# Attention backward core on one core: head-0 scores issued one unit ahead into the spare PSUM bank, and the transposes and projections moved from even to odd units

## Chip, cores, metric

The kernel runs on one core of a Trainium2 chip. The metric is the device time of one execution in microseconds (us), as the median of several executions. Engines are named as in the profile: PE is TensorE, ACT is ScalarE, DVE is VectorE, POOL is GpSimd, and SP issues DMAs. A ratio between two kernels is the mean time of one kernel's fast runs over that of the other's fast runs of the same rounds, so it isn't quite the ratio of the medians quoted beside it.

## Reference

Two attention blocks share one call; the reference returns the output and all gradients. Only the second block (B) matters here: multi-query attention with 16 query heads, one key/value head, and head width 28 (padded to 32 in the kernel).

```python
def _B_ref(x, wq, wk, wv, wo):               # B, S, D = 1, 2048, 448; H = 16; Dh = 28
    q = (x @ wq).reshape(B, S, H, Dh).transpose(0, 2, 1, 3)
    k = x @ wk                                # one head, shared
    v = x @ wv
    scores = jnp.einsum("bhqd,bkd->bhqk", q, k) * (Dh ** -0.5)
    p = softmax(scores)
    o = jnp.einsum("bhqk,bkd->bhqd", p, v)
    return o.transpose(0, 2, 1, 3).reshape(B, S, H * Dh) @ wo
# ... block A (linear attention) ...
_out, _vjp = jax.vjp(_f, ...)                 # output and eight gradients, bfloat16
```

## The kernel before

Block B's core is a loop over 512 units and 28 more to drain it. Eight units make a *group*: 256 query rows times two heads, against all 2048 keys; a unit takes 256 keys. In unit `u` the forward part works on unit `u` (scores, exp) and the backward part on unit `w = u - 16` (dP, dS). Scores have three PSUM banks (`SB`; a bank is a 128x512 piece of the memory that PE writes its results to), used in rotation: two for the two heads of a unit, and one spare. dP has two (`DB`). In the profile they are called `sps` and `dps`. Names with d are gradients: dq, dk, dv and do those of q, k, v and the head output o, dP and dS those of the probabilities and the scores.

```python
def rows_SD(u, sp, dp):                       # scores (k=0) and dP (k=1), two heads, two halves each
    # ...
    todo = [(0, 0), (0, 1), (1, 0), (1, 1)] * 2
    if sp is not None and dp is not None and u % 2 == 0:
        todo = [(0, 0), (0, 1), (1, 0)] * 2 + [(1, 1)] * 2
    # ... each one is a matmul of 32 rows x 128 columns, on row group r

def out_part(u):
    n, q_ = (u % 64 - 24) // 8, u // 64 - 1   # a quarter of an output projection in some units 0 mod 8
    # ...

for u in range(NU + 28):                      # program order is issue order on each engine
    sp = [SB[(2 * u + h) % 3] for h in range(2)] if hasS else None
    dp = DB if hasD else None
    spare = SB[(2 * u + 2) % 3] if hasS else SB[2]
    rows_SD(u, sp, dp)
    if (b := due(u, 10)) is not None:         # units 2 mod 8
        onat_T(b, spare)                      # transposes of o into the spare bank
    if (b := due(u, 14)) is not None:         # units 6 mod 8
        don_T(b, spare)                       # transposes of do
    if op := out_part(u):
        out_proj(*op, spare)                  # projection
    # ... do projections in some units, also into the spare bank
    ACT:  exp head 0 -> eT
    DVE:  dsT head 0 = dP head 0 * eT;  ACT: cp = copy(dP head 1);  POOL: dsT head 1 = cp * eT
    # ... DVE and POOL read the transposes out: o_norm, row_D, don_copy, out_store
    ACT:  exp head 1 -> eT;  every second unit: SP: DMA transpose eN <- eT
    if u % 2:
        dk_m(...)                             # 16 matmuls, odd units
    else:
        o_dq(...)                             # o and dq, even units
        for n in {4: (0,), 6: (1, 2), 0: (3,)}.get(u % 8, ()):
            dv_mm(...)                        # dv, reads eN
    DVE:  dsx <- transpose(dsT)
```

The three names ACT, DVE and POOL in front of a line are shorthand of this text for the engine call that stands there. "Extra" below means any of the things that use the spare bank: transposes of o, transposes of do, a projection.

## Time and profile before

| | before |
|---|---|
| time, median of 4 runs | 1110.22 us (1110.05 to 1111.34) |
| first exp of unit 0, of unit 64, of unit 511 | 227.3, 332.7, 1027.9 us |
| units 64 to 511 | 695.1 us |
| one group (8 units) late in the core, with / without a projection | 12.56 / 12.19 us |

The unit times are worked out from the starts of the exp of head 0 in the timeline (ACT instruction of line 861). The averages of the last row are over units 192 to 503.

The page's head and part 1 give the span and each engine's busy time, share and instruction count:

```profile
span 1106.9 us, 39147 instructions
...
PE 1044.4 (94%) x15645; PEld 484.3 (44%) x15645; DVE 897.9 (81%) x1772; ACT 881.4 (80%) x1744; POOL 757.3 (68%) x986
```

The timeline of ACT, one group, only the exp of head 0 of units 304 to 312 (columns: start in us, duration in us, engine, line, instruction, and in brackets the idle time before it and what ended it). Between two shown lines stand the copy and the exp of head 1.

```profile
707.70 0.62 ACT L861 ACTIVATE eT<-sps 128x512 bf16<-128x512 f32 x1
...
709.55 0.60 ACT L861 ACTIVATE eT<-sps 128x512 bf16<-128x512 f32 x1 [0.25 <-PE dps L625]
...
711.00 0.62 ACT L861 ACTIVATE eT<-sps 128x512 bf16<-128x512 f32 x1
...
712.68 0.60 ACT L861 ACTIVATE eT<-sps 128x512 bf16<-128x512 f32 x1
...
714.12 0.62 ACT L861 ACTIVATE eT<-sps 128x512 bf16<-128x512 f32 x1
...
715.72 0.60 ACT L861 ACTIVATE eT<-sps 128x512 bf16<-128x512 f32 x1
...
717.17 0.62 ACT L861 ACTIVATE eT<-sps 128x512 bf16<-128x512 f32 x1
...
718.86 0.60 ACT L861 ACTIVATE eT<-sps 128x512 bf16<-128x512 f32 x1
...
720.30 0.62 ACT L861 ACTIVATE eT<-sps 128x512 bf16<-128x512 f32 x1
```

Read the differences. From an odd to an even unit it is 1.45 us each time: ACT starts its three instructions 0.48 us apart and waits for nothing. From an even to an odd unit it is 1.85 us after a projection (707.70 to 709.55), 1.68 after the transposes of o, 1.60 with no extra, 1.69 after the transposes of do. The bracket names a dP matmul: the profile puts the wait down to the last matmul of the set, and the score matmuls stand just before it in the same set.

Why even to odd is longer can be seen in the timeline of PE, in unit 306, with its transposes of o (line 744; `oq` is the bank of o and dq):

```profile
710.43 0.28 PE L625 MATMUL sps<-R,R 32*128 32x256 bf16 x2
...
710.55 0.50 PE L625 MATMUL dps<-doT,R 32*128 32x256 bf16 x3
711.18 0.33 PE L744 MATMUL sps<-identF,oTs 64*128 64x64 f32 x2
711.44 0.29 PE L625 MATMUL oq<-eT,R 128*32 128x256 bf16 x2
...
712.26 0.28 PE L625 MATMUL sps<-R,R 32*128 32x256 bf16 x2 [0.21 <-DVE oTs L754]
```

The transposes start at 711.18 although the rows of the unit were issued by 710.8: they wait for the spare bank, which the exp of head 1 of the unit before still reads until 711.12. Then come the transposes (0.26 us to the next start), o and dq, and a wait of 0.21 us until DVE has read the transposes out. Only then can the next unit's scores (712.26) use that bank, and ACT gets them 0.42 us later. An extra in an even unit is thus a chain: release of the bank, extra, o and dq, next scores. Which end of it binds differs: after the transposes of o, it is DVE's read-out (it ends at 1.22 us from the unit's exp, the scores start at 1.27; medians of units 192 to 503); after the other two extras DVE is done 0.2 us before the scores start, so PE's own work (o, dq and dv) is taken to bind.

The waits from 250 to 1030 us (who waited for whom, total us, times, longest):

```profile
PEld sps L744 <- ACT eT L899: 24.7, 62, 0.4
ACT eT L861 <- PE dps L625: 18.9, 45, 6.9
PE sps L625 <- DVE oTs L754: 13.2, 61, 0.5
...
PE dv_acc L625 <- DMA eN<-eT: 6.5, 1, 6.5
```

The last line is a single stall of 6.5 us: the first dv matmuls wait for a DMA transpose. The busy times by stretch show it and what follows (columns: stretch, its length, busy us and count of each engine, granted PE clock, DMA share, GB/s):

```profile
257.00:260.00 3.00, 0.26 (x7) 0.00 (x0) 1.05 (x3) 1.03 (x3) 2.22 (x3) 1.00 1.69 113
260.50:267.50 7.00, 3.73 (x45) 1.64 (x48) 2.28 (x5) 2.57 (x6) 1.15 (x1) 0.51 1.04 185
```

PE is idle, and from 260.5 us, still inside the stall, it gets half its clock for 7 us. The Trainium skill, "TensorE: Matmul & The Clock Gate" (Part 1: The HAM clock gate), says that the clock is halved after an idle window of about 3.4 us and returns after about as long a busy one; here the stall is longer than such a window and the clock reads 0.51.

### The profile page before, as it was taken

The numbers are of one execution on the slowest core, as the hardware profiler recorded it, in microseconds if no ns is written. First come the engines' busy times: TensorE is split into PE (matmuls) and PEld (weight loads), VectorE is DVE, ScalarE is ACT, GpSimd is POOL, SyncE is SP. The second block draws the span as 40 slices with busy tenths as digits, with TensorE's granted clock in tenths as the row PEclk, the third lists the DMA queues.
The fourth block names the chain that finished last, engine by engine and source line by source line (L and its number), as shares of the span: only waits on it lengthen the run. The fifth ranks groups of instructions, "written<-read, shape, count | busy, mean of one in ns | idle before, by whom it ended". The sixth has DMA issues, their size and how long they took to land.

```text
span 1106.9 us, 39147 instructions
## 1 busy us (share of the span) xinstructions
PE 1044.4 (94%) x15645; PEld 484.3 (44%) x15645; DVE 897.9 (81%) x1772; ACT 881.4 (80%) x1744; POOL 757.3 (68%) x986
## 2 busy tenths in 40 slices
PE   9999999997999999999999999999999999999998
PEld 5545555443444444444444444444444444444344
DVE  7886400436999999999999999999999999999942
ACT  6454122567999999999999999999999999999621
POOL 6001252325888888888888888888888888888840
PEclk9999999988999999999999999999999999999999
DMA  9869899199999999999999999999999999999962
GB/s 267 143 131 185 176 181 216 39 200 168 192 192 191 187 188 199 187 187 189 180 192 191 185 184 187 192 191 190 187 204 186 178 185 192 194 171 178 206 138 63
DMA packets 672535, 199.01 MB, mean 180 GB/s; under 512 B 649585, under 2 KB 668321, under 8 KB 672353
## 3 DMA queue, kind: packets, MB, share of 16 engines
q1 hardware_dynamic: 660512, 175.19, 98.2%
q0 software_dynamic: 6880, 17.37, 6.5%
q10 hardware_dynamic: 4960, 3.96, 1.2%
q8 instruction: 122, 2.00, 0.7%
q14 instruction: 61, 0.49, 0.1%
HBM read 21.00 MB, written 12.94 MB: 31 GB/s over the span
## 4 chain that ended last, share of the span: by engine, by line
PE 53%; DVE 29%; ACT 7%; issue 6%; DMA 4%; POOL 0%; SPq 0%; DVEq 0%; ACTq 0%; POOLq 0%
PE agen L80 13%; PE dk_acc L625 11%; DVE dsx L931 11%; DVE dsT L866 9%; PE sps L80 6%; ACT eT L899 5%; PE oq L625 5%; PE sps L625 4%; PE aacc L80 4%; PE dps L625 3%; PE dv_acc L625 3%; DVE R L884 2%; DVE oTs L881 2%; DMA eN<-eT 2%; DVE oTs L754 2%
## 5 line engine op out<-in xcount | busy, mean ns | idle before, releaser
L869 POOL TENSOR_TENSOR dsT<-cp,eT 128x512 bf16<-128x512 bf16 x512 | 588.1, 1155 | 122.1 <-ACT cp L868 114.6
L866 DVE TENSOR_TENSOR dsT<-dps,eT 128x512 bf16<-128x512 f32 x512 | 343.4, 671 | 27.8 <-PE dps L625 22.7
L931 DVE STREAM_TRANSPOSE dsx<-dsT 128x512 f32<-128x512 f32 x512 | 357.7, 699 | 2.1
L861 ACT ACTIVATE eT<-sps 128x512 bf16<-128x512 f32 x512 | 311.8, 609 | 37.4 <-PE dps L625 18.9
L625 PEld LDWEIGHTS <-R 32*128 32x128 bf16 (+1 forms) x8192 | 197.9, 94 | 304.5 <-issue 272.5
L868 ACT ACTIVATE cp<-dps 128x512 bf16<-128x512 f32 x512 | 312.8, 611 | 11.5 <-PE dps L625 10.4
L899 ACT ACTIVATE eT<-sps 128x512 bf16<-128x512 f32 x512 | 319.0, 623 | 0.0
L625 PE MATMUL dk_acc<-dsx,qX 32*32 32x512 bf16 x4096 | 267.6, 375 | 0.0
L625 PE MATMUL dps<-doT,R 32*128 32x256 bf16 x2048 | 252.7, 270 | 13.0 <-DVE dsT L866 7.7
L625 PE MATMUL sps<-R,R 32*128 32x256 bf16 x2048 | 217.5, 274 | 14.9 <-DVE oTs L754 13.2
L625 PE MATMUL oq<-eT,R 128*32 128x256 bf16 x2048 | 158.3, 276 | 0.0
L625 PE MATMUL oq<-dsT,R 128*32 128x256 bf16 x2048 | 157.5, 275 | 0.1
L625 PEld LDWEIGHTS <-qX 32*32 32x32 bf16 x4096 | 79.7, 89 | 114.8 <-issue 54.2
L625 PE MATMUL dv_acc<-eN,don 128*32 128x512 bf16 x1024 | 96.9, 379 | 6.5 <-DMA eN<-eT 6.5
L80 PEld LDWEIGHTS <-R 128*128 128x128 bf16 (+1 forms) x553 | 45.8, 99 | 46.1 <-issue 18.7
L396 POOL MEMSET ga<- 64x448 bf16 x2 | 0.9, 470 | 93.4 <-DVE pr L347 80.0
L546 DVE TENSOR_TENSOR osb<-R 32x512 bf16<-32x512 bf16 x4 | 1.6, 412 | 62.1 <-ACT R L543 62.1
L625 PEld LDWEIGHTS <-don 128*32 128x32 bf16 x1024 | 33.8, 97 | 0.3
L80 PE MATMUL agen<-R,R 128*128 128x448 bf16 x128 | 28.6, 352 | 0.7 <-ACT R L219 0.5
L874 POOL DMA_DIRECT2D qX<-qn_d x32 | 18.1, 569 | 16.4 <-PE dps L80 16.4
L884 DVE TENSOR_SCALAR R<-oq 64x256 bf16<-64x256 f32 x64 | 27.3, 427 | 2.0
L499 ACT ACTIVATE wdq<-agen 128x448 bf16<-128x448 f32 x16 | 8.7, 543 | 24.9 <-PE agen L80 24.9
(220 smaller groups left out, 1023.5 us busy)
## 6 DMA issues: line engine op xcount, KB each, us to landing
qX<-qn_d POOLq DMA_DIRECT2D x32, 256.0 KB, 6.2
eN<-eT SPq DMA_TRANSPOSE x256
out_dram<-osb ACTq DMA_DIRECT2D x22, 112.0 KB
qn_d<-gaT SPq DMA_DIRECT2D x2, 1024.0 KB
xa<-in_A_x_dram SPq DMA_DIRECT2D x8, 224.0 KB
ga<-in_grad_out_dram SPq DMA_DIRECT2D x4, 448.0 KB
xa<-in_grad_out_dram POOLq DMA_DIRECT2D x4, 448.0 KB, 6.9
out_dram<-wdq POOLq DMA_DIRECT2D x8, 224.0 KB, 3.6
```

The lines of the kernel that those rows point to most:

```text
L80: nc.tensor.matmul(out_ap, lhsT=lhsT, rhs=rhs, start=start, stop=stop, tile_position=(0, 0))
L625: nc.tensor.matmul(out, lhsT=lhsT, rhs=rhs, start=start, stop=stop, tile_position=pos, skip_group_check=True)
L754: nc.vector.tensor_tensor(out=os_, in0=onp[:, :, :, :], in1=r_[:].to_broadcast([P, 2, 2, 32]), op=ALU.mult)
L861: nc.scalar.activation(out=et[:, u % 2, 0, :], in_=sp[0][:, :], func=ACT.Exp, scale=scale)
L866: nc.vector.tensor_tensor(out=dst[:, 0, :], in0=dp[0][:, :], in1=ew[:, w % 2, 0, :], op=ALU.mult)
L868: nc.scalar.activation(out=cp[:, :], in_=dp[1][:, :], func=ACT.Copy)
L869: nc.gpsimd.tensor_tensor(out=dst[:, 1, :], in0=cp[:, :], in1=ew[:, w % 2, 1, :], op=ALU.mult)
L874: nc.gpsimd.dma_start(qX[qc][32 * a:32 * a + 32, :, :, :].rearrange("j b s c -> j b (s c)"), qn_d[qc * 256:(qc + 1) * 256, :].rearrange("( ...
L881: nc.vector.tensor_copy(out=oTs[0:64, :], in_=oq[0:64, 0:256])
L884: nc.vector.tensor_scalar(out=qT_B[g][64 * hp:64 * hp + 64, qc * 256:(qc + 1) * 256], in0=oq[64:128, 0:256], scalar1=scale, scalar2=None, ...
L899: nc.scalar.activation(out=et[:, u % 2, 1, :], in_=sp[1][:, :], func=ACT.Exp, scale=scale)
L931: nc.vector.transpose(out=dsx[b][:, tp, :, :, :].rearrange("p h t c -> p (h t c)").bitcast(F32), in_=dsT[y][:, :, :].rearrange("p h c -> p ...
```

## The change

Intent: while an even unit runs, the head-0 scores of the next, odd unit are put into the spare bank, so ACT always has an exp to do when PE is late. The spare bank must then be free in even units, so everything else that uses it moves to odd units. The early loads of qX and wo and the do projections are re-timed as well.

```diff
-        def rows_SD(u, sp, dp):
+        def rows_SD(u, sp, dp, early, ahead):
+            todo = []
+            if sp is not None:
+                todo += [(0, u, 1)] if early else [(0, u, 0), (0, u, 1)]
+            if dp is not None:
+                todo += [(1, w, 0), (1, w, 1)]
+            todo *= 2
+            if dp is not None and sp is not None and u % 2 == 0:
+                todo = [d for d in todo if d != (1, w, 1)] + [(1, w, 1)] * 2
+            if ahead is not None:
+                todo += [(0, u + 1, 0)] * 2
... (out_part: units 1 mod 8 instead of 0 mod 8)
-        free = [*range(1, 16), *range(17, 27, 2), *range(32, 64, 8), ...]
+        free = [*range(1, 16), *range(17, 27, 2), *range(29, 65, 4), 65, 69, 73]
...
-                rows_SD(u, sp, dp)
-                if (b := due(u, 10)) is not None:
+                op = out_part(u)
+                dpj = do_slots.pop(u, None)
+                taken = op or due(u, 11) is not None or due(u, 15) is not None or dpj is not None and u >= 27
+                ahead = spare if u + 1 < NU and not taken else None
+                rows_SD(u, sp, dp, early, ahead)
+                early = ahead is not None
+                if (b := due(u, 11)) is not None:
                     onat_T(b, spare)
-                if (b := due(u, 14)) is not None:
+                if (b := due(u, 15)) is not None:
                     don_T(b, spare)
...
-                for a in {2: (0, 2), 8: (1, 3)}.get(u, ()) ...      # first qX loads
+                for a in {10: (0, 2), 18: (1, 3)}.get(u, ()) ...
-                if u == 12:
+                if u == 44:
                     nc.gpsimd.dma_start(wo, ...)
... (row_D 12 -> 13, o_norm 10 -> 11, don_copy 14 -> 15; the qT copy after o_norm)
```

Units 3 (o) and 7 (do) mod 8 are always taken, and unit 1 mod 8 where a projection falls in. In those units no early score is issued.

## The prediction

> **What bounds it now.** The attention core (512 units, first exp of unit 0 at 227 us, of unit 511 at 1028 us) is 800 of 1110 us. In the timeline a unit is three ScalarE instructions (exp head 0, copy, exp head 1), started 0.48 us apart: 1.45 us per unit, 11.6 us per eight units. Measured: 12.5-12.66 us per eight with an output projection, 12.13-12.24 without. TensorE sets the difference. The unit-to-unit intervals show it: odd to even is always 1.45 us (ScalarE-bound), even to odd is 1.68 (after the transposes of o), 1.70 (of do), 1.88 (projections): the extra work in an even unit delays the next unit's first scores. Besides, the waits list one stall of 6.5 us near 257 us: the first dv matmuls wait for transposing DMAs, while four qX loads and the wo load share the DMA engines.
>
> **What the change does, costed.**
> (a) Even units are always "ahead", so even to odd falls to about 1.45-1.55 us. Gain in eight units: about 0.6 us, 1.0 with a projection.
> (b) Extras now stand in odd units, before the dk matmuls, and take the spare bank, so there is no early score for the next unit. That bank is released by exp head 1 of the unit before, 0.19 us after the unit's own first exp starts. Then run: extra (0.26 o; about 0.35 do with one more mode switch; 0.47 projection), dk 0.975, scores to exp 0.43. Odd to even becomes about 1.85, 2.0-2.1 and 2.06 us instead of 1.45. Loss: 1.0 us in eight units, 1.6 with a projection. In even units only o/dq followed (0.45-0.55), not dk.
> (c) The early scores wait, in TensorE's order, for exp head 1 of the unit before. TensorE now leads ScalarE by 0.4-0.7 us; in odd "ahead" units it will stand still about 0.4-0.5 us and start the next extra later. Two serial matmuls on one row group also add 0.1 us per ahead unit.
> (d) Half of the first qX loads and wo are issued later: most of the 6.5 us stall goes.
>
> The Trainium skill, "TensorE: Matmul & The Clock Gate" (The mechanism), says that matmuls keep strict order: this is why (c) blocks. "TensorEngine Tiling" (Key Properties) says that changing tiling mode drains the engine: the trace agrees, with about 0.2 us between rows, transposes and dk.
>
> Following these waits by hand through eight units reproduces before (12.08 against 12.13-12.24) and gives after about 12.8 us without and 13.3 with a projection (estimates from the durations above). Over 62 such groups that is +36 to +41 us, less 5-6 us for (d).
>
> **Predicted: 1142 us, range 1114 to 1162; faster by over 2%: 0.14, within 2%: 0.22, slower by over 2%: 0.64.**
>
> **What would show each step.** (a) Even-to-odd intervals near 1.45-1.55. (b) Odd-to-even intervals of 1.85-2.1 at the extras, with ScalarE's first exp waiting for scores there; 1.45 elsewhere. (c) In the waits, TensorE's score matmuls waiting for the head-1 exp, tens of us in total; the projections and transposes of o waiting for it too. (d) No 6.5 us dv wait near 257 us.
>
> **What would make it wrong.** If TensorE falls behind ScalarE for good, the early scores never block and the gain (a) dominates: at TensorE's own sum of about 11.8-12.3 us per eight, the time is near 1085. If the do transposes need no extra switch, the loss shrinks. If the eT-to-eN transposing DMAs, which are up to 18 us late early on, bind, less changes. VectorE (about 11.3 us of 12.5 occupied) could also hide part.

## The result

| | before | after |
|---|---|---|
| time, median of 4 runs | 1110.22 us | 1143.12 us (1141.21 to 1144.3) |
| ratio of fast runs, 95% interval | | 1.0292 [1.0275, 1.031] |
| first exp of unit 0 | 227.3 | 229.5 |
| units 0 to 64 | 105.4 | 106.5 |
| units 64 to 511 | 695.1 | 726.6 |
| rest to the end | 79.0 | 79.9 |
| one group, with / without a projection | 12.56 / 12.19 | 13.29 / 12.67 |

Nearly all of the loss, 31.5 us of 35.7 us between the two profiled runs, lies in units 64 to 511: 0.72 us in each group with a projection and 0.48 without (averages over units 192 to 503).

Units 0 to 64 took 1.1 us longer, but that is a sum of larger parts. The third group, which had a DMA stall before, gained 7.0 us; the five groups after it lost 5.9; and the first group lost 2.3 (14.19 us against 11.88). In that first group PE got half its clock for 13.6 us, against 6.9 before. This length varies from trace to trace (3.4 us in four of the twelve, 6.8 in six, 10.3 and 13.6 in one each), and the first group takes 10.7, 11.9 to 12.1, 13.0 and 14.2 us with it. So the 2.3 us can't be put down to the change.

The page's head and part 1 of the kernel after:

```profile
span 1142.6 us, 38986 instructions
...
PE 1099.7 (96%) x15645; PEld 510.1 (45%) x15645; DVE 913.5 (80%) x1772; ACT 879.6 (77%) x1744; POOL 760.6 (67%) x986
```

PE, the engine with the higher share, became busier by 55 us with the same number of matmuls. That isn't 55 us of new work: durations are modelled and overlapping ones are merged here. Matmuls that used to run side by side (dP and both scores) now stand partly one behind the other, but that can't be all of it: the run without early scores further below, where no scores are put ahead, is still at 1070.3 us, 26 more than before. The busy time of PE therefore doesn't tell what the change costs; the unit times do.

The timeline of ACT, the same units 304 to 312, exp of head 0 (now line 870):

```profile
727.03 0.60 ACT L870 ACTIVATE eT<-sps 128x512 bf16<-128x512 f32 x1 [0.38 <-PE dps L625]
...
728.48 0.62 ACT L870 ACTIVATE eT<-sps 128x512 bf16<-128x512 f32 x1
...
730.58 0.60 ACT L870 ACTIVATE eT<-sps 128x512 bf16<-128x512 f32 x1 [0.50 <-PE dps L625]
...
732.03 0.62 ACT L870 ACTIVATE eT<-sps 128x512 bf16<-128x512 f32 x1
...
733.93 0.60 ACT L870 ACTIVATE eT<-sps 128x512 bf16<-128x512 f32 x1 [0.30 <-PE dps L625]
...
735.38 0.62 ACT L870 ACTIVATE eT<-sps 128x512 bf16<-128x512 f32 x1
...
738.34 0.60 ACT L870 ACTIVATE eT<-sps 128x512 bf16<-128x512 f32 x1
...
740.31 0.60 ACT L870 ACTIVATE eT<-sps 128x512 bf16<-128x512 f32 x1 [0.38 <-PE dps L625]
```

Now even to odd is 1.45 us, as intended. (The first experiment shows that moving the extras out of the even units is enough for that; the early scores aren't needed.) (Unit 310, at 736.81, is left out by the cut, so 735.38 to 738.34 are two units.) But odd to even after an extra is 2.10 (projection), 1.90 (o), 1.97 (do). Averages over units 192 to 503, in us, groups with a projection:

| from unit to unit, mod 8 | 0-1 | 1-2 | 2-3 | 3-4 | 4-5 | 5-6 | 6-7 | 7-0 | sum |
|---|---|---|---|---|---|---|---|---|---|
| before | 1.84 | 1.45 | 1.69 | 1.45 | 1.53 | 1.45 | 1.70 | 1.45 | 12.56 |
| after | 1.45 | 2.10 | 1.45 | 1.91 | 1.45 | 1.43 | 1.53 | 1.97 | 13.29 |

The timeline of PE in unit 307, which has the transposes of o (now line 749), answers to the one of unit 306 before; the last three lines are unit 309, which has early scores and is read further below:

```profile
731.73 0.36 PE L625 MATMUL dps<-doT,R 32*128 32x256 bf16 x2
732.21 0.34 PE L749 MATMUL sps<-identF,oTs 64*128 64x64 f32 x2
732.48 1.04 PE L625 MATMUL dk_acc<-dsx,qX 32*32 32x512 bf16 x16
733.45 0.28 PE L625 MATMUL sps<-R,R 32*128 32x256 bf16 x2
...
735.24 0.28 PE L625 MATMUL dps<-doT,R 32*128 32x256 bf16 x2
735.55 0.37 PE L625 MATMUL sps<-R,R 32*128 32x256 bf16 x2
735.86 0.61 PE L625 MATMUL dk_acc<-dsx,qX 32*32 32x512 bf16 x8
```

Behind the transposes stands dk with 0.97 us instead of o and dq with about 0.5 us and a wait of 0.2. From the start of the transposes to the next scores it was 1.08 us; it is 1.24 us. ACT gets the scores at 733.93, 0.48 us after their start.

The waits from 250 to 1062 us:

```profile
ACT eT L870 <- PE dps L625: 54.3, 148, 0.5
...
PEld sps L749 <- ACT eT L908: 23.9, 62, 0.4
...
PE dps L625 <- DVE dsT L875: 3.2, 15, 0.2
```

ACT's wait for PE grew from 18.9 us in 45 waits (of which 6.9 were the DMA stall) to 54.3 in 148. The wait of dv for the DMA is gone, and so is the half clock in that stretch:

```profile
257.00:260.00 3.00, 2.76 (x30) 1.40 (x30) 2.71 (x7) 3.00 (x8) 2.37 (x3) 1.00 1.27 169
260.50:267.50 7.00, 6.45 (x106) 3.13 (x109) 6.69 (x14) 6.70 (x14) 6.92 (x11) 1.00 1.11 189
```

The third group (units 16 to 24) takes 12.36 us instead of 19.40.

### The profile page after: what moved, and what is told of

It reads as the page before. It is cut to its first block, busy times and chain, and to the rows that moved or that the text cites. A ratio compares the mean times of both kernels' runs of the same rounds, so it can differ in the third digit from the quotient of the medians.

```text
span 1142.6 us, 38986 instructions
## 1 busy us (share of the span) xinstructions
PE 1099.7 (96%) x15645; PEld 510.1 (45%) x15645; DVE 913.5 (80%) x1772; ACT 879.6 (77%) x1744; POOL 760.6 (67%) x986
## 4 chain that ended last, share of the span: by engine, by line
PE 62%; ACT 15%; DVE 13%; issue 8%; DMA 1%; DVEq 0%; ACTq 0%
PE dk_acc L625 17%; PE agen L80 12%; PE sps L625 10%; ACT cp L877 6%; ACT eT L908 6%; PE sps L80 5%; DVE dsx L940 5%; PE aacc L80 4%; DVE dsT L875 4%; PE oq L625 3%; PE dps L625 3%; PE dv_acc L625 2%; DVE R L899 2%; PE dps L80 2%; ACT eT L870 1%
## 5 line engine op out<-in xcount | busy, mean ns | idle before, releaser
L875 DVE TENSOR_TENSOR dsT<-dps,eT 128x512 bf16<-128x512 f32 x512 | 350.1, 684 | 54.2 <-PE dps L625 45.8
L625 PEld LDWEIGHTS <-R 32*128 32x128 bf16 (+1 forms) x8192 | 222.0, 94 | 334.7 <-issue 318.0
L870 ACT ACTIVATE eT<-sps 128x512 bf16<-128x512 f32 x512 | 314.4, 614 | 64.5 <-PE dps L625 54.3
L877 ACT ACTIVATE cp<-dps 128x512 bf16<-128x512 f32 x512 | 310.8, 607 | 12.5 <-PE dps L625 12.3
L625 PE MATMUL sps<-R,R 32*128 32x256 bf16 x2048 | 311.0, 273 | 8.1 <-DVE R L586 0.8
L625 PE MATMUL dps<-doT,R 32*128 32x256 bf16 x2048 | 225.2, 271 | 12.8 <-DVE dsT L875 4.5
L625 PE MATMUL dv_acc<-eN,don 128*32 128x512 bf16 x1024 | 90.9, 379 | 0.0
L80 PEld LDWEIGHTS <-R 128*128 128x128 bf16 (+1 forms) x553 | 46.1, 100 | 46.5 <-issue 18.9
L763 POOL TENSOR_TENSOR prod<-R,oTs 128x128 f32<-128x128 bf16 x64 | 27.7, 433 | 2.0 <-DVE oTs L759 2.0
L625 PEld LDWEIGHTS <-don 128*32 128x32 bf16 x1024 | 28.1, 97 | 0.6
```

The costliest lines, as they stand in the source:

```text
L80: nc.tensor.matmul(out_ap, lhsT=lhsT, rhs=rhs, start=start, stop=stop, tile_position=(0, 0))
L625: nc.tensor.matmul(out, lhsT=lhsT, rhs=rhs, start=start, stop=stop, tile_position=pos, skip_group_check=True)
L763: nc.gpsimd.tensor_tensor(out=prod[b][:], in0=dnv, in1=os_, op=ALU.mult)
L870: nc.scalar.activation(out=et[:, u % 2, 0, :], in_=sp[0][:, :], func=ACT.Exp, scale=scale)
L875: nc.vector.tensor_tensor(out=dst[:, 0, :], in0=dp[0][:, :], in1=ew[:, w % 2, 0, :], op=ALU.mult)
L877: nc.scalar.activation(out=cp[:, :], in_=dp[1][:, :], func=ACT.Copy)
```

## The experiments

The theory: the loss is made by the place of the extras (dk now stands behind them), with a smaller part by the early scores, which wait in PE's order. Rival A: the early scores make it all. Rival B: the early scores help, and the place loses more than the whole. The runs below were made on two chips, each with the kernel before beside it. In them, the kernel before itself scatters (1103.7 to 1118.3 us in seven fast runs of the first call, the longest with the lowest mean granted clock, 0.987), so time ratios under about 1% don't say much. The unit intervals inside a trace do: where a kernel's instructions were the same, their averages agreed with those of the first pair within 0.03 us, mostly within 0.01. The table of unit times at the end of this section uses them.

### The change without its early scores

```diff
-                ahead = spare if u + 1 < NU and not taken else None
+                ahead = None
```

> The change without its early scores: transposes and projections stay in odd units. My theory (loss shared by position of the extras and early scores): following the waits gives 12.9 us in eight units with a projection and 12.3 without, about 0.3 less than the change, so 1122 to 1128 us; odd-to-even intervals at the extras still 1.8 to 2.1 us. Rival A (the early scores make the whole loss): 1102 to 1108 us. Rival B (the position makes the loss, and the early scores win some of it back): slower than the change, 1150 us or more.

Measured: 1135.2 us against 1107.34 of before, ratio 1.0233 [1.0182, 1.0284]; correct. The intervals at the extras are 2.10 (projection), 1.90 (o) and 1.84 (do), nearly those of the change; a group takes 13.19 and 12.57 us. The time missed the expected 1122 to 1128 us. The timeline of ACT, the exp of head 0 of units 305 to 308 (between them stand the copy and the exp of head 1):

```profile
722.74 0.61 ACT L870 ACTIVATE eT<-sps 128x512 bf16<-128x512 f32 x1
...
724.83 0.60 ACT L870 ACTIVATE eT<-sps 128x512 bf16<-128x512 f32 x1 [0.50 <-PE dps L625]
...
726.29 0.61 ACT L870 ACTIVATE eT<-sps 128x512 bf16<-128x512 f32 x1
...
728.17 0.60 ACT L870 ACTIVATE eT<-sps 128x512 bf16<-128x512 f32 x1 [0.29 <-PE dps L625]
```

Even to odd (724.83 to 726.29) is short here too: 1.46, 1.46, 1.51 and 1.48 us on average.

So the place of the extras alone costs 0.63 and 0.38 us per group, and the early scores 0.10 on top (13.29 less 13.19, 12.67 less 12.57). Rival A falls. Rival B falls too, since taking the early scores out made it no slower: units 64 to 511 take 721.3 us against 726.6. (The two time ratios to before, 1.0233 and 1.0292, are too close for their intervals to settle this.) The theory's split was wrong in size: about 0.3 was expected for the early scores, and 0.3 less for the place of the extras.

### Before, with the early scores only

```diff
+                taken = op or due(u, 10) is not None or due(u, 14) is not None or dpj is not None and u >= 27
+                ahead = spare if u + 1 < NU and not taken else None
+                rows_SD(u, sp, dp, early, ahead)          # rows_SD of the change; extras stay in even units
```

> Before, with early scores wherever the spare bank is free; extras stay in even units. My theory: the early scores alone lose, by standing in TensorE's order until the head-1 exp has read the bank and by two serial matmuls: 12.8 us in eight units with a projection, 12.65 without, so 1128 to 1136 us. Rival A (early scores make the whole loss): 1140 us or more. Rival B (early scores help): 1110 us or less.

Measured: 1120.58 us, ratio 1.0103 [1.0048, 1.0157]; correct. A group takes 12.69 us with and 12.63 without a projection, against 12.56 and 12.19. Early scores lose by themselves, by 0.13 and 0.44 us per group, less in time than expected. Part of the difference may be that the profiled run had no long stall near 257 us (0.7 us, against 6.5 in before's trace), although its loads were the old ones.

Here the early scores stand in odd units and make the *next*, even unit with its extra start later: the interval 6 to 7 is 1.93 us instead of 1.70 and, in groups without a projection, 2 to 3 is 2.07 instead of 1.66.

### Half of dk left out, in both kernels (result wrong)

```diff
-                        for m in range(2 * i, 2 * i + 4):
+                        for m in (2 * i, 2 * i + 3):
                             dk_m(b, m)
```

In the change:

> The change with every second dk matmul group left out (the dk result is wrong on purpose); dk takes 0.43 us less in each odd unit. If the dk stretch stands between an extra and the next scores (my theory), the odd-to-even intervals at the extras shrink by that: projection 2.10 to about 1.67, o transposes 1.91 to 1.48, do transposes 1.97 to 1.54, all others stay near 1.45; about 12.0 us in eight units with a projection and 11.8 without, near 1076 us. Rival (the stall is the wait for the bank and its eviction, or ScalarE itself): these intervals stay within 0.1 us.

In the kernel before:

> Before with the same half of dk left out (dk wrong on purpose). My theory: before, dk ends ahead of the even unit and is hidden behind ScalarE, and the extra then waits for the bank (head-1 exp), so the even-to-odd intervals at the extras stay within 0.1 us of 1.84 (projection), 1.69 (o), 1.70 (do): 12.3 to 12.6 and 11.9 to 12.2 us in eight units, at most 12 us faster than before. Rival (TensorE's total work binds both kernels): about 1.7 us less in eight units, 100 us faster.

Measured: the change with half of dk 1110.08 us against 1111.18 of before, ratio 1.000 [0.9948, 1.0053]; the kernel before with half of dk 1104.57 us, 0.9951 [0.9898, 1.0003]. Only one output was wrong in both, the gradient of wk, which is made from dk. The change with half of dk missed its expectation (near 1076 us).

| | units 64 to 511, us | 1-2 (projection) | 3-4 (o) | 7-0 (do) |
|---|---|---|---|---|
| after | 726.6 | 2.10 | 1.91 | 1.97 |
| after, half of dk | 699.9 | 1.85 | 1.66 | 1.99 |
| | | 0-1 (projection) | 2-3 (o) | 6-7 (do) |
| before | 695.1 | 1.84 | 1.69 | 1.70 |
| before, half of dk | 695.2 | 1.85 | 1.70 | 1.70 |

This is the sharpest of the runs. The same 0.43 us less of dk per odd unit is worth 26.7 us in the change and nothing before. Before, dk stood where PE had time to spare; the change put it between an extra and the scores that ACT waits for.

But the theory's sizes were wrong: in groups with a projection, the projection and o intervals fell by 0.25, not 0.43 (o in the other groups by 0.16), and do didn't fall. In the half-dk run the waits from 300 to 1030 us have a line that the change doesn't have:

```profile
PE sps L625 <- DVE doT L787: 14.8, 53, 0.4
```

With dk shorter, the next scores wait until DVE has copied the transposed do out of the bank. In the change, dk hid that. The same bound stands behind the other two extras, though the waits don't list it: in the half-dk run the next scores start 0.05 us after DVE's read-out has ended (projection: 1.38 and 1.33 us from the unit's exp; o: 1.19 and 1.13; medians of units 192 to 503), in the change 0.3 us after it.

### Half of dk, with the copy of do ahead of the multiply on DVE

```diff
                 if (b := due(u, 15)) is not None:
                     don_T(b, spare)
+                    don_copy(b)              # taken from its place after the dsT multiply
```

> The change with half of dk (wrong on purpose), and VectorE copies the transposed do out before the unit's dsT multiply instead of after it. In the half-dk run the interval 7 to 0 stayed at 1.94 to 1.99 us while the other two fell by 0.25. If that is because the eviction of do by VectorE, which stands behind the multiply, holds the bank (so dk hid it in the change), the interval falls to 1.5 to 1.65 us. Rival: something else holds unit 0's scores (dO multiply, don on GpSimd), it stays at 1.9 or more.

Measured: 1118.74 us, ratio 1.0083 [1.0035, 1.0131]. The expectation was missed: interval 7 to 0 rose to 2.15 us. The timeline of units 311 and 312, all engines, shows why:

```profile
725.89 0.28 DVE L787 COPY doT<-sps 64x256 bf16<-64x256 bf16 x1 [0.51 <-PE sps L780]
...
726.10 0.67 DVE L876 TENSOR_TENSOR dsT<-dps,eT 128x512 bf16<-128x512 f32 x1
...
726.25 0.10 PEld L625 LDWEIGHTS <-R 32*128 32x128 bf16 x3 [0.43 <-issue]
726.25 0.28 PE L625 MATMUL sps<-R,R 32*128 32x256 bf16 x2
...
726.82 0.26 PE L625 MATMUL dps<-doT,R 32*128 32x256 bf16 x1 [0.29 <-DVE dsT L876]
...
727.19 0.60 ACT L871 ACTIVATE eT<-sps 128x512 bf16<-128x512 f32 x1 [0.42 <-PE dps L625]
```

The copy ends at 726.17 and the first half of the scores starts at 726.25, so the bank no longer holds them. But the multiply now ends late, at 726.77. The first dP matmul needs its bank and waits until 726.82, and the second half of the scores stands behind it in PE's order. DVE has both things to do between two sets of rows, and the order only chooses which of them PE waits for. So the do interval has a second bound close under dk, made of two DVE instructions.

### Before, with the later loads only

```diff
-                for a in {2: (0, 2), 8: (1, 3)}.get(u, ()) ...
+                for a in {10: (0, 2), 18: (1, 3)}.get(u, ()) ...
-                if u == 12:
+                if u == 44:
```

> Before, with only the later qX and wo loads of the change. My theory (part d): the 6.5 us wait of the first dv matmuls near 257 us goes, nothing else moves, so 5 to 7 us faster than before: 1103 to 1105 us. Rival: the wait only moves to the next user of the late loads (dk at unit 27), so within 2 us of before.

Measured: 1109.49 us, ratio 1.0006 [0.9946, 1.0067]: not settled. In its trace the third group took 12.90 us instead of 19.40, and units 0 to 64 took 100.5 us instead of 105.4. But later groups of the same stretch grew (14.03 us for units 48 to 56, after the moved wo load), and the run above with the old loads and early scores had no such stall either (13.05 us for the third group). The stall thus depends on more than these loads. The other traces help: none of the eight with the later loads (the change and seven runs) has a wait of dv for the DMA over 0.25 us between 245 and 285 us, and the four with the old loads have 6.5, 4.3, 3.3 and 0.7. So the later loads go with its absence, but what they are worth in time stays open. In units 64 to 511 they change nothing clear (695.8 us against 695.1), so they are no rival for the loss there.

### One dv step moved to a unit without an extra

```diff
-                    for n in {4: (0,), 6: (1, 2), 0: (3,)}.get(u % 8, ()):
+                    for n in {4: (0, 1), 6: (2,), 0: (3,)}.get(u % 8, ()):
```

> Before, with one of the two dv groups of units 6 mod 8 moved to units 4 mod 8, which have no extra. If TensorE's work in a pair of units that has an extra is what binds (my theory), the interval 6 to 7 falls from 1.70 to about 1.59 or less and nothing else grows: 12.3 us in eight units with a projection and 11.9 without, 10 to 14 us faster than before, 1096 to 1100 us. Rival: the interval 6 to 7 is bound by the wait for don or by another engine, no change.

Measured: 1109.6 us, ratio 0.9992 [0.9932, 1.0053]. The interval 6 to 7 fell from 1.70 to 1.50, and a group took 12.39 us with and 12.03 without a projection (medians, which leave the disturbed groups out): PE's work beside that extra was what bound, as the theory said. Yet the time didn't move, because of a line in its waits from 250 to 1040 us, which before has once at 6.5 us:

```profile
PE dv_acc L625 <- DMA eN<-eT: 12.0, 4, 4.3
```

At the faster pace the DMA transposes came too late four times. The longest, 4.3 us, is the old stall near 262 us; the other three begin about 7 us after a load of qX. In the two longest (4.3 and 3.6 us) the granted clock halved again (0.5 from 265 to 271 and from 732 to 739 us in the clock records). Three further versions went after this.

With the later loads as well:

> Before with one dv group moved to units 4 mod 8 and with the later qX and wo loads. The moved group alone took 0.2 us off each eight units, but the dv matmuls then waited for the transposing DMAs four times, 12 us in all. If the late loads at the head cause that lateness, they go and the time is 1093 to 1100 us; if the transposing DMAs have no room at this pace at all, waits at units after qX loads stay and the time is 1100 to 1110 us.

Measured: 1106.42 us, ratio 0.9977 [0.9922, 1.0032]. PE again stood idle before dv matmuls, up to 4.6 us, at about 313, 430, 630 and 731 us; the profile puts the last three down to the DMA transposes. The trace is that of the slowest of the four runs (1114.33 us).

With the later loads and a changed rotation of the banks after the transposes of o, so that the next head-0 scores take the bank already read, and the head-1 scores, which take the other, come last:

> As the run with the moved dv group and the later loads, and after the o transposes the next unit's head 0 takes the bank that is already read instead of the bank under eviction: the interval 2 to 3 falls from 1.69 to about 1.5. Without DMA waits 12.1 us in eight units with a projection and 11.8 without, 1082 to 1092 us; if the transposing DMAs bind (about 3 us each, 12 us in eight units), no faster than the run before it.

Measured: 1109.23 us, ratio 0.9997 [0.9931, 1.0064]. The interval 2 to 3 fell to 1.48 us as expected, but 3 to 4 (1.56) and 4 to 5 (1.63 or more) grew by as much: the medians of a group stayed at 12.38 us with and 12.02 without a projection. In this trace too dv waited for the DMA, 10.0 us in all.

With each qX load of 0.5 MB split into two, twelve units apart:

```diff
-                for a in {2: (0, 2), 8: (1, 3)}.get(u, ()) or {38: (0, 2), 54: (1, 3)}.get(u % 64, ()) * (u < 448):
+                loads = {10: (0, 2), 18: (1, 3)}.get(u, ())
+                if u > 20:
+                    loads = {38: (0,), 50: (2,), 62: (1,)}.get(u % 64, ()) * (u < 448) or (3,) * (u % 64 == 10 and 64 < u < 460)
+                for a in loads:
-                if u == 12:
+                if u == 68:
                     nc.gpsimd.dma_start(wo, ...)
```

> Before with one dv group moved to units 4 mod 8, the head loads later, wo at unit 68, and each qX load of 0.5 MB split into two of 0.25 MB 12 units apart. If the dv waits on the transposing DMAs come from the bursts of qX, they go and the gain of 0.2 us in eight units remains: 1090 to 1098 us, faster than before by about 1%. If the transposing DMAs have no room at this pace, waits remain and it is within 0.5% of before.

Measured: 1103.35 us against 1109.3, ratio 0.9929 [0.9894, 0.9964]; correct. One of its six runs and one of before's eleven were slow and are left out of the ratio. This version beats both kernels, by about 0.7% over before. In its trace the wait of dv for the DMA from 250 to 1030 us is

```profile
PE dv_acc L625 <- DMA eN<-eT: 2.2, 3, 1.1
```

so the bursts made most of the lateness, as far as one trace can show it (the wo load was moved as well). The gain is less than the 1% expected: units 64 to 511 took 691.4 us, only 3.7 less than in before's trace, and some groups still take 13.2 us. Part of what is gained is lost at the end, which takes 84.6 us after unit 511 instead of 79.0: PE waits 2.8 us for a load of the gradient, and then has half its clock for 6.9 us.

### Units 64 to 511 in all traces that the verdict rests on

| kernel | units 64 to 511, us | against before |
|---|---|---|
| before | 695.1 | |
| early scores only | 708.6 | +13.5 |
| extras in odd units, no early scores | 721.3 | +26.1 |
| the change (both) | 726.6 | +31.5 |
| the change, half of dk | 699.9 | +4.8 |
| before, half of dk | 695.2 | +0.1 |
| before, later loads only | 695.8 | +0.7 |
| dv moved, loads spread | 691.4 | -3.7 |

The early scores cost 13.5 us alone and 5.3 on top of the moved extras, so the two parts don't simply add. Not tried: the extras in odd units with dk moved to even ones, which would test the place of dk with a right result.

## Why the prediction was right

**The time and the sum per group.** 1142 us was predicted and 1143.12 measured; 12.8 and 13.3 us per group were predicted, and 12.67 and 13.29 measured. The main mechanism, dk standing between an extra and the next scores, was right, and it was followed wait by wait with durations from the trace of before. But the close sum is luck in part. The same arithmetic without the early scores gave 12.3 and 12.9 us, and 12.57 and 13.19 were measured: it made the place of the extras too cheap by 0.3 us per group and the early scores too dear by 0.2, and the two errors nearly cancelled.

**(a) Even to odd falls to 1.45-1.55.** Right in number: 1.45, 1.45, 1.45 and 1.53 us. The reason given, that even units are always "ahead", isn't what does it: without early scores it is 1.46, 1.46, 1.51 and 1.48. The gain comes from the extras having left the even units.

**(b) Odd to even grows to 1.85 (o), 2.0-2.1 (do), 2.06 (projection).** Right within 0.06: 1.91, 1.97 and 2.10 us. The runs show the cause: much the same intervals come without the early scores (1.90, 1.84, 2.10), and half of dk gives back 26.7 us in the change and nothing before. The prediction's chain "extra, dk, scores" was incomplete: the reading out of the bank by DVE runs beside dk and is nearly as long. A shorter dk gave 0.25 of 0.43 us for o and projection, and nothing for do. And the do interval was met by two errors that cancel: the term "about 0.35" for the do transposes "with one more mode switch" was too large, since from the first transposing matmul to dk it is 0.22 us in the trace (725.36 to 725.58); but these transposes start 0.29 us after the unit's exp and not 0.19, because the rows ahead of them are late (medians: 0.29, against 0.17 in the run without early scores).

**(c) The early scores block PE.** Right in kind, too large in weight, and with a wrong signature. The last three lines of the timeline of PE of the kernel after, shown in the result, are unit 309 and show the blocking. The early scores start at 735.55, 0.05 us after the exp of head 1 of unit 308 has ended (734.90 and 0.60 long), 0.3 us after the matmuls ahead of them. The prediction said that the waits would list "tens of us in total" for score matmuls. They list none, because the modelled durations of the matmuls ahead cover all but 0.02 us of the gap; only the transposes of o are listed (23.9 us, and 24.7 before). By the run without early scores the whole of (c) is worth 0.10 us per group, where the arithmetic gave about 0.3. It is paid mostly where (c) said, at the start of the next extra: the interval after the do transposes is 1.97 us with early scores and 1.84 without. The early scores also help in one place: the interval 4 to 5 is 1.45 us with them and 1.51 without. The Trainium skill, "TensorE: Matmul & The Clock Gate" (The mechanism), states strict order of the matmuls; the traces agree, most plainly in the copy-first run, where half of the scores wait 0.6 us behind a dP matmul that they don't need.

**(d) Most of the 6.5 us stall goes.** The trace after agrees (third group 12.36 us instead of 19.40). The later loads go with it in all eight traces that have them, but one run with the old loads had hardly any stall either, and the run with them alone gave no clear time. In units 0 to 64 the 7.0 us gained there are more than used up: the first group lost 2.3 us in a longer stretch at half the clock, which the prediction didn't foresee, and the five groups after the third lost 5.9.

**Mode switches.** The Trainium skill, "TensorEngine Tiling" (Key Properties), says that a change of tiling mode drains the engine. The traces fit this: from the last matmul of a set of rows to the first of another mode it is about 0.2 us, and from one step of the rows to the next, in the same mode, 0.12 us.

## What to carry to other kernels

Look-ahead bought nothing here, where the look-ahead buffer must be given up exactly in the steps that are late; count what stands between the release of that buffer and the work the waiting engine needs. When moving a piece of work to another step, ask what stands *behind* it there: 0.97 us of dk behind an extra cost more than 0.5 us of o and dq. And shortening the suspected stretch in both kernels, even with a wrong result, tells whether it is on the critical path in one, the other or both: here it was 26.7 us against 0.1. Last, a sum that comes out right doesn't show that its terms are right: the runs that take one part out did that.

## What the Trainium skill lacked or had wrong

- "ScalarE: Activation LUTs" (What ACT_TABLE_LOAD costs) says that back-to-back ACTIVATEs overlap by about 93 ns. Here instructions of 0.60 to 0.62 us start 0.48 us apart, so they overlap by 0.12 to 0.14 us.
- "TensorEngine Tiling" (Key Properties) gives no figure for the drain of a mode switch. The runs show about 0.2 us from start to start across a switch, against 0.12 us within a mode, for matmuls of 256 columns.
- No page that was read says that a matmul blocked by a semaphore may hardly show as a wait in the profile. Here two starts lie 0.31 us apart where 0.12 is usual, and the profile leaves a gap of 0.02 us: the modelled durations of the matmuls ahead cover the rest.
- "TensorE: Matmul & The Clock Gate" (Part 1: The HAM clock gate) says that the full clock comes after at least one busy window of about 3.4 us, and not when it takes more than one. At the start of the core here, the half clock lasted 3.4, 6.8, 10.3 or 13.6 us depending on the trace; in the longest, the profile has PE busy for all but 0.1 of 14.0 us.
